# Batches 1 to 3 of a retention kernel: k-v products column-tiled, and the state by one scan per head pair

## The chip, the cores and the metric

One core of a Trainium2 chip runs the kernel. The metric is the device time in microseconds (us), as a median over runs. The profile is one execution of the same program, taken by the hardware profiler; its span goes from the first to the last instruction.

## The reference

Inputs are q, k, v of shape (4 batches, 8 heads, 768 steps, 64), and two weights of 512x2048 and 2048x512. All arithmetic of the reference is in float32.

```python
gamma = 1.0 - 2.0 ** (-5.0 - np.arange(H))
for t in range(S):
    state = gamma[None, :, None, None] * state + np.einsum('bhd,bhe->bhde', k[:, :, t], v[:, :, t])
    y[:, :, t] = scale * np.einsum('bhd,bhde->bhe', q[:, :, t], state)
x = y.transpose(0, 2, 1, 3).reshape(B, S, H * D)
X = np.fft.fft(np.fft.fft(x, axis=1), axis=2)
u = x + np.real(X)
un = (u - u.mean(-1, keepdims=True)) / np.sqrt(u.var(-1, keepdims=True) + 1e-06)
out = u + np.maximum(un @ w_ch1, 0.0) @ w_ch2
```

So there is a decayed linear attention ("retention"), a Fourier mix over steps and channels, a normalisation, and a feed-forward with a ReLU.

## The kernel before

**Tiles.** The 768 steps are cut into NCH = 6 chunks of 128. Two heads form a pair; a batch has four pairs, taken in the order of `PAIR_ORDER`. Within a chunk the attention is computed as a masked product; from chunk to chunk goes a state of 64x64 per head. The kernel works in float16 with float32 sums in PSUM.

**One pair of a later batch (1, 2, 3)** goes through these units, which are Python closures, one after the other over successive steps of `attn_steps`:

- `cast_unit`: GpSimd (in batches 2 and 3 ScalarE for q) casts q, k and v to float16; k is scaled by the decay within its chunk (`kd`).
- `kv_unit`: for chunks 0 to 4, the product of kd and v (128 steps contracted), then the running state `s16`, in which each chunk's product is added to gamma^128 times the state before. TensorE and VectorE (DVE) work here, lines 579 to 597.
- `t_unit`: q and k are transposed, by TensorE in batch 1 and by DMA transposes in batches 2 and 3. qT is zero-padded: for each head, the 64 rows of the other head of the pair are zero.
- `a_unit`: k times q per chunk (line 566), then the mask with its decay on DVE (line 568).
- `y_unit`: per head, q times the state of the chunk before (line 615) and the masked product times v (line 619) add up in one PSUM tile; ScalarE scales it into `x` (line 627).

`kv_unit` is emitted one step after the casts and `y_unit` one step after that. The folds (`fold_s`, `fold_d`), the two stages of the Fourier mix (`s1_unit`, `s2_unit`), the normalisation (`norm_unit`, `unT_unit`) and the feed-forward (`h_unit` line 855 and its ReLUs in lines 859 and 861; `ch_unit` line 892 and its last step in line 896) follow.

**The first batch** has units of its own. There, `kv0_unit` computes the products column-tiled: each head has a half of TensorE's columns, and writes 64 of the 128 PSUM partitions. It puts the chunk index innermost, so that the products of one element over five chunks lie side by side in PSUM. `sc_unit` then makes all five states with one `tensor_tensor_scan`; its factors lie in `gk5`, filled by `gk_unit` for all four pairs, with a zero at chunk 0, at which the scan starts afresh. `yx_unit` (line 492) reads the state with a stride of five, row-tiled: each head uses 64 of the array's rows.

**Order.** While the feed-forward of batch b runs, the attention of batch b + 1 is emitted beside it: `emit` merges streams of units by a position between b and b + 1. The first batch is pinned in its order by `pin`; of the later ones only GpSimd's early instructions are, and the framework's scheduler settles the order of the other engines' instructions from estimated costs. Across the first batch, `filler` (line 139) puts dummy matmuls between the units.

**Buffers.** `ps_g` gives five PSUM buffers of one bank to products, transposes, masked products, y and the Fourier stages. `ps_pm` has three, for the feed-forward. `s16` has two buffers in SBUF, kd three, v16 four.

Of the kernel before, what the change touches and what calls it, by code (L numbers as in the profile page):

```python
# [12 lines left out]
ALU = mybir.AluOpType  # L13
f32 = mybir.dt.float32
f16 = mybir.dt.float16
# [3 lines left out]
P = 128  # L19
B, H, S, D = 4, 8, 768, 64  # L20
DM = 512
DFF = 2048
NCH = S // P
# [6 lines left out]
PAIR_ORDER = [0, 1, 3, 2]  # L30
# [4 lines left out]
def kernel(  # L35
# [9 lines left out]
    nc = tc.nc  # L45
# [3 lines left out]
    def pool(name, bufs, **kw):  # L49
        return ctx.enter_context(tc.tile_pool(name=name, bufs=bufs, **kw))  # L50
# [7 lines left out]
    sp = pool("sp", 2)  # L58
# [8 lines left out]
    ps_g = pool("ps_g", 5, space=PSUM)  # L67
# [3 lines left out]
    ps_pm = None  # L71
# [11 lines left out]
    gkrow = const.tile([P, NHP, NCH - 1], f32, tag="gkrow")  # L83
    gk5 = const.tile([P, NHP, D, NCH - 1], f32, tag="gk5")
# [101 lines left out]
    for h in range(H):  # L186
# [6 lines left out]
                            op0=ALU.mult)  # L193
# [262 lines left out]
    def sc_unit(i):  # L456
        def run():
            st = at[0, i]
            st["s16"] = sp.tile([P, D, NCH - 1], f16, tag="s16", name="s16",
                                padded_shape=[P, P, NCH - 1])  # L460
            nc.vector.tensor_tensor_scan(
                out=st["s16"].rearrange("p e c -> p (e c)"),
                data0=gk5[:, PAIR_ORDER[i]].rearrange("p e c -> p (e c)"),
                data1=st["wkf"], initial=0.0, op0=ALU.mult, op1=ALU.add)
        return run
# [108 lines left out]
    def kv_unit(b, i):  # L574
        def run():
            st = at[b, i]
            hp = PAIR_ORDER[i]
            kd, v16 = kd_of[b, i], v16_of[b, i]
            s16 = sp.tile([P, NCH - 1, P], f16, tag="s16", name="s16")
            st["s16"] = s16  # L580
            for c0, n in ((0, 3), (3, 2)):
                wk = ps_g.tile([P, 3, P], f32, tag="g", name="wkK", padded_shape=[P, 4, P])
                for c in range(c0, c0 + n):
                    nc.tensor.matmul(wk[:, c - c0, :], kd[:, c].rearrange("p a b -> p (a b)"),
                                     v16[:, c].rearrange("p a b -> p (a b)"),
                                     start=True, stop=True)
                for c in range(c0, c0 + n):
                    if c == 0:
                        if b == 0:
                            nc.scalar.copy(s16[:, 0], wk[:, 0])  # L590
                        else:
                            nc.vector.tensor_copy(s16[:, 0], wk[:, 0])
                    else:
                        nc.vector.scalar_tensor_tensor(out=s16[:, c], in0=s16[:, c - 1],  # L594
                                                       scalar=gkrow[:, hp, 1:2],
                                                       in1=wk[:, c - c0],
                                                       op0=ALU.mult, op1=ALU.add)
        return run

    def y_unit(b, i):  # L600
        def run():
            st = at.pop((b, i))
            hp = PAIR_ORDER[i]
            v16, s16, atm, qT = v16_of[b, i], st["s16"], st["atm"], st["qT"]
            ypool, ytag = (ps_pm, "pm") if b == 0 else (ps_g, "g")
            yk = [ypool.tile([P, NCH, D], f32, tag=ytag, name="wkY", padded_shape=[P, 8, D])
                  for _ in range(2)]
            for c in range(1, NCH):
                for h2 in range(2):
                    sl = slice(64 * h2, 64 * h2 + 64)  # L610
                    if b == 0:
                        lhsT, rhs = qT[sl, c, :], s16[sl, c - 1, sl]
                    else:
                        lhsT, rhs = qT[:, h2, c, :], s16[:, c - 1, sl]
                    nc.tensor.matmul(yk[h2][:, c, :], lhsT, rhs,
                                     start=(c == 1), stop=False, skip_group_check=True)
            for h2 in range(2):
                for c in range(NCH):
                    nc.tensor.matmul(yk[h2][:, c, :], atm[:, c, h2, :], v16[:, c, h2, :],  # L619
                                     start=False, stop=(c == NCH - 1), skip_group_check=True)  # L620
                h = 2 * hp + h2
                x = xts[b % 2]
                if h < 4:
                    dst = x[:, :, 0, 64 * h + 1:64 * h + 65]
                else:
                    dst = x[:, :, 1, 513 - 64 * h:449 - 64 * h:-1]
                nc.scalar.activation(dst, yk[h2], AF.Copy, bias=0.0, scale=gq8[:, h:h + 1])  # L627
        return run
# [390 lines left out]
    ps_pm = pool("ps_pm", 3, space=PSUM)  # L1019
    late_consts()  # L1020
    streams = []
    for b in range(B):
# [17 lines left out]
        if b + 1 < B:  # L1040
# [6 lines left out]
            else:  # L1047
                streams.append(([load_unit(b + 1, i) for i in range(4)], b - 0.3, b + 0.15))
                n = [len(u) for u in steps]
# [40 lines left out]
```

## Time and profile before

| | |
|---|---|
| median of 3 runs | 263.74 us (262.87 to 264.59) |
| the profiled execution's own time | 263.17 us |
| its span | 261.5 us |
| granted TensorE clock, mean | 0.997 |
| PE busy | 241.9 us (93%) |
| DVE busy | 182.9 us (70%) |
| ACT busy | 117.5 us (45%) |
| POOL busy | 72.7 us (28%) |

PE is TensorE, DVE is VectorE, ACT is ScalarE, POOL is GpSimd; PEld is the loading of weights into TensorE, beside its matmuls. L594 is line 594 of the kernel. In a group of instructions, the tiles written stand before the arrow and the tiles read after it, then the shape, the count, the busy time in us with the mean duration in ns, and the idle time of the engine just before with what ended it. Matmuls overlap: the duration of one is its time from start to end, while the next may start much earlier, so what a matmul costs TensorE is the distance from its start to the next one's. A row of the timeline merges instructions of one line; its second number reaches from the first start to the last end.

### The profile page before, as it was taken

The numbers are of one execution on the slowest core, as the hardware profiler recorded it, in microseconds if no ns is written. First come the engines' busy times: TensorE is split into PE (matmuls) and PEld (weight loads), VectorE is DVE, ScalarE is ACT, GpSimd is POOL, SyncE is SP. The second block draws the span as 40 slices with busy tenths as digits, with TensorE's granted clock in tenths as the row PEclk, the third lists the DMA queues.
The fourth block names the chain that finished last, engine by engine and source line by source line (L and its number), as shares of the span: only waits on it lengthen the run. The fifth ranks groups of instructions, "written<-read, shape, count | busy, mean of one in ns | idle before, by whom it ended". The sixth has DMA issues, their size and how long they took to land.

```text
span 261.5 us, 5242 instructions
## 1 busy us (share of the span) xinstructions
PE 241.9 (93%) x2024; PEld 146.1 (56%) x2024; DVE 182.9 (70%) x446; ACT 117.5 (45%) x242; POOL 72.7 (28%) x129
## 2 busy tenths in 40 slices
PE   6897899989998989799999999899999999999993
PEld 2454778756766536465566546555556455545541
DVE  7999857878999775898777726897687637523421
ACT  7877677653652346653144406551245305402200
POOL 6658301586100081570001603550002203100000
PEclk9999999999999999999999999999999999999998
DMA  8998999999999109999990294686110431211012
GB/s 177 265 247 136 204 202 213 228 241 260 270 225 216 46 0 236 170 201 188 260 235 2 41 173 122 129 112 131 43 40 0 53 116 35 43 66 55 0 43 80
DMA packets 97432, 35.99 MB, mean 138 GB/s; under 512 B 88192, under 2 KB 94336, under 8 KB 97408
## 3 DMA queue, kind: packets, MB, share of 16 engines
q1 hardware_dynamic: 93184, 31.47, 58.9%
q0 software_dynamic: 4224, 4.19, 9.9%
q8 instruction: 16, 0.26, 0.4%
q14 instruction: 8, 0.07, 0.1%
HBM read 27.26 MB, written 6.29 MB: 128 GB/s over the span
## 4 chain that ended last, share of the span: by engine, by line
PE 48%; DVE 18%; ACT 9%; DMA 9%; POOL 7%; SPq 4%; issue 3%; POOLq 0%; ACTq 0%
PE psc L892 19%; PE psh L855 16%; DMA qTz<-q16z 4%; SPq L153 4%; POOL u L795 3%; ACT x L627 3%; DVE bst L811 3%; DVE atm L568 3%; PE ps L685 2%; DMA unT<-un 2%; DMA k<-in_k_dram 2%; DVE xab L644 2%; PE wkA L566 2%; DVE ht L861 2%; POOL u L793 2%
## 5 line engine op out<-in xcount | busy, mean ns | idle before, releaser
L892 PE MATMUL psc<-w,ht 128*128 128x512 f16 x384 | 89.7, 379 | 0.0
L855 PE MATMUL psh<-unT,w 128*128 128x384 f16 x448 | 82.7, 326 | 2.0 <-ACT ht L859 1.1
L855 PEld LDWEIGHTS <-w 128*128 128x128 f16 x448 | 42.5, 98 | 26.2 <-issue 3.3
L892 PEld LDWEIGHTS <-ht 128*128 128x128 f16 x384 | 36.4, 98 | 36.7
L859 ACT ACTIVATE ht<-psh 128x384 f16<-128x384 f32 x56 | 27.4, 488 | 54.3 <-PE psh L855 54.3
L793 POOL TENSOR_TENSOR u<-u,x 128x256 f32<-128x256 f32 x21 | 13.3, 635 | 126.6 <-DVE u L786 123.0
L861 DVE TENSOR_SCALAR ht<-psh 128x384 f16<-128x384 f32 x56 | 30.8, 550 | 12.1 <-PE psh L855 11.8
L896 DVE SCALAR_TENSOR_TENSOR ob<-psc,stats,u 128x512 f32<-128x512 f32 x24 | 17.9, 746 | 25.9 <-PE psc L892 25.8
L568 DVE TENSOR_TENSOR atm<-wkA,maskp 128x512 f16<-128x512 f32 x36 | 23.6, 680 | 2.0 <-PE wkA L566 2.0
L627 ACT ACTIVATE x<-wkY,gexp 128x384 f16<-128x384 f32 x24 | 12.8, 580 | 22.7 <-PE wkY L619 22.6
L813 ACT ACTIVATE un<-u,stats 128x512 f16<-128x512 f32 x21 | 15.1, 720 | 15.8 <-DVE stats L812 13.0
L811 DVE BATCH_NORM_STATS2 bst<-u 128x6 f32<-128x512 f32 x21 | 14.6, 694 | 9.4 <-POOL u L795 9.3
L594 DVE SCALAR_TENSOR_TENSOR s<-s,gkrow,wkK 128x128 f16<-128x128 f16 x48 | 16.3, 339 | 1.1
L139 PE MATMUL wps<-ht 128*128 128x512 f16 x44 | 14.4, 434 | 2.2 <-POOL ht L184 2.2
L566 PE MATMUL wkA<-qTz,kT 128*128 128x256 f16 x72 | 12.6, 272 | 3.1 <-DMA qTz<-q16z 2.9
L349 POOL TENSOR_SCALAR kd<-k,gexp 128x384 f16<-128x384 f32 x24 | 13.7, 583 | 1.7 <-DMA k<-in_k_dram 1.7
L795 POOL TENSOR_TENSOR u<-u,x 128x256 f32<-128x256 f32 x21 | 13.3, 634 | 2.4 <-DVE u L788 1.3
L786 DVE SCALAR_TENSOR_TENSOR u<-pq,g,qn 128x257 f32<-128x257 f32 x24 | 11.4, 474 | 3.5 <-ACT qn L783 3.5
L872 PE MATMUL psh<-unT,w 128*128 128x128 f16 x192 | 11.4, 219 | 0.4 <-ACT unT L846 0.2
L566 PEld LDWEIGHTS <-kT 128*128 128x128 f16 x72 | 6.8, 97 | 8.6 <-issue 4.6
L783 ACT COPY qn<-pq 128x255 f32<-128x255 f32 x24 | 8.8, 369 | 6.2 <-PE pq L774 5.4
L872 PEld LDWEIGHTS <-w 128*128 128x128 f16 x192 | 11.0, 98 | 0.8 <-issue 0.7
(142 smaller groups left out, 314.5 us busy)
## 6 DMA issues: line engine op xcount, KB each, us to landing
q<-in_q_dram SPq DMA_DIRECT2D x16, 384.0 KB, 6.0
k<-in_k_dram SPq DMA_DIRECT2D x16, 384.0 KB, 5.7
v<-in_v_dram SPq DMA_DIRECT2D x16, 384.0 KB, 6.3
out_dram<-ob SPq DMA_DIRECT2D x24, 256.0 KB, 2.2
w<-in_moe_w_ch_dram POOLq DMA_DIRECT2D x8, 512.0 KB, 11.1
unT<-un SPq DMA_TRANSPOSE x12, 2.5
kT<-kd SPq DMA_TRANSPOSE x8, 3.1
qTz<-q16z SPq DMA_TRANSPOSE x8, 3.8
```

Source lines behind the costliest of these rows:

```text
L566: nc.tensor.matmul(wk[:, c2], st["kT"][:, c, :], st["qT"][:, :, c, :], start=True, stop=True)
L568: nc.vector.tensor_tensor(out=st["atm"][:, 2 * part:2 * part + 2], in0=wk, in1=maskp[:, PAIR_ORDER[i]].unsqueeze(1).to_broadcast([P, 2, 2, ...
L627: nc.scalar.activation(dst, yk[h2], AF.Copy, bias=0.0, scale=gq8[:, h:h + 1])
L793: nc.gpsimd.tensor_tensor(out=u[:, kb, 0:256], in0=u[:, kb, 0:256], in1=x[:, kb, 0, 1:257], op=ALU.add)
L795: nc.gpsimd.tensor_tensor(out=u[:, kb, 256:512], in0=u[:, kb, 256:512], in1=x[:, kb, 1, 257:1:-1], op=ALU.add)
L811: nc.vector.bn_stats(bst, u[:, kb, :])
L855: nc.tensor.matmul(psh, w116[:, cb, fb * P:(fb + 1) * P], unT[:, cb, rt * 384:(rt + 1) * 384], start=(cb == 0), stop=(cb == 3))
L859: nc.scalar.activation(ht16[:, fb, :], psh, AF.Relu, bias=0.0, scale=-1.0)
L861: nc.vector.tensor_scalar(out=ht16[:, fb, :], in0=psh, scalar1=-1.0, scalar2=0.0, op0=ALU.mult, op1=ALU.max)
L872: nc.tensor.matmul(psh[:, f], w116[:, cb, fb * P:(fb + 1) * P], unT[:, cb, kb * P:(kb + 1) * P], start=(cb == 0), stop=(cb == 3))
L892: nc.tensor.matmul(psc, ht16[:, fb, rb3 * P:(rb3 + 1) * P], w216[:, fb, :], start=(fb == 0), stop=(fb == NFB - 1))
L896: nc.vector.scalar_tensor_tensor(out=ob, in0=psc, scalar=lb[b]["st"][:, rb, 3:4], in1=lb[b]["u"][:, rb, :], op0=ALU.mult, op1=ALU.add)
```

## The change

For batches 1 to 3, `kv_unit` now does what `kv0_unit` and `sc_unit` do. Ten matmuls per pair (five chunks, two heads) of 128 rows by 64 columns with 64 moving columns go column-tiled into one PSUM tile of [128, 64, 5]; before, five matmuls of 128x128 with 128 moving columns went into two PSUM tiles, in which only the diagonal blocks were of use. One scan makes the state `s16` as [128, 64, 5]; before, it was a copy and four `scalar_tensor_tensor` steps into [128, 5, 128]. `y_unit` reads `s16[:, :, c - 1]`, 64 columns with a stride of five elements; before, it read 64 contiguous ones, `s16[:, c - 1, sl]`. The stationary side, the zero-padded qT, is as it was. Branches for batch 0, which these units do not serve, are taken out, and so is the padding of `s16` in the first batch.

```diff
@@ sc_unit
             st["s16"] = sp.tile([P, D, NCH - 1], f16, tag="s16", name="s16",
-                                padded_shape=[P, P, NCH - 1])
+)
@@ kv_unit
-            hp = PAIR_ORDER[i]
             kd, v16 = kd_of[b, i], v16_of[b, i]
-            s16 = sp.tile([P, NCH - 1, P], f16, tag="s16", name="s16")
-            st["s16"] = s16
-            for c0, n in ((0, 3), (3, 2)):
-                wk = ps_g.tile([P, 3, P], f32, tag="g", name="wkK", padded_shape=[P, 4, P])
-                for c in range(c0, c0 + n):
-                    nc.tensor.matmul(wk[:, c - c0, :], kd[:, c].rearrange("p a b -> p (a b)"),
-                                     v16[:, c].rearrange("p a b -> p (a b)"),
-                                     start=True, stop=True)
-                for c in range(c0, c0 + n):
-                    if c == 0:
-                        if b == 0:
-                            nc.scalar.copy(s16[:, 0], wk[:, 0])
-                        else:
-                            nc.vector.tensor_copy(s16[:, 0], wk[:, 0])
-                    else:
-                        nc.vector.scalar_tensor_tensor(out=s16[:, c], in0=s16[:, c - 1],
-                                                       scalar=gkrow[:, hp, 1:2],
-                                                       in1=wk[:, c - c0],
-                                                       op0=ALU.mult, op1=ALU.add)
+            wkf = ps_g.tile([P, D * (NCH - 1)], f32, tag="g", name="wkK", padded_shape=[P, DM])
+            wk = wkf.rearrange("p (e c) -> p e c", c=NCH - 1)
+            for c in range(NCH - 1):
+                for h2 in range(2):
+                    nc.tensor.matmul(wk[D * h2:D * h2 + D, :, c], kd[:, c, h2, :],
+                                     v16[:, c, h2, :], start=True, stop=True)
+            st["s16"] = sp.tile([P, D, NCH - 1], f16, tag="s16", name="s16")
+            nc.vector.tensor_tensor_scan(
+                out=st["s16"].rearrange("p e c -> p (e c)"),
+                data0=gk5[:, PAIR_ORDER[i]].rearrange("p e c -> p (e c)"),
+                data1=wkf, initial=0.0, op0=ALU.mult, op1=ALU.add)
@@ y_unit
-            ypool, ytag = (ps_pm, "pm") if b == 0 else (ps_g, "g")
-            yk = [ypool.tile([P, NCH, D], f32, tag=ytag, name="wkY", padded_shape=[P, 8, D])
+            yk = [ps_g.tile([P, NCH, D], f32, tag="g", name="wkY", padded_shape=[P, 8, D])
                   for _ in range(2)]
             for c in range(1, NCH):
                 for h2 in range(2):
-                    sl = slice(64 * h2, 64 * h2 + 64)
-                    if b == 0:
-                        lhsT, rhs = qT[sl, c, :], s16[sl, c - 1, sl]
-                    else:
-                        lhsT, rhs = qT[:, h2, c, :], s16[:, c - 1, sl]
-                    nc.tensor.matmul(yk[h2][:, c, :], lhsT, rhs,
+                    nc.tensor.matmul(yk[h2][:, c, :], qT[:, h2, c, :], s16[:, :, c - 1],
                                      start=(c == 1), stop=False, skip_group_check=True)
```

## The prediction

> **What bounds the kernel now.** I read the page first, then the busy time by stage, then the waits of TensorE, then the groups of instructions, and last the timeline of TensorE around single units.
>
> ```profile
> PE 241.9 (93%) x2024; PEld 146.1 (56%) x2024; DVE 182.9 (70%) x446; ACT 117.5 (45%) x242; POOL 72.7 (28%) x129
> ```
>
> TensorE is busy for 93% of the span. An average says little about the stages that the edit touches, so I cut out the three in which attention of batches 1, 2 and 3 runs beside the feed-forward of the batch before (columns: stretch, its length, busy us and instructions of PE, PEld, DVE, ACT, POOL).
>
> ```profile
> 60.00:100.00 40.00, 37.83 (x340) 23.47 (x338) 33.55 (x79) 16.84 (x32) 9.46 (x15) 1.00 0.81 164
> 100.00:140.00 40.00, 37.77 (x335) 23.89 (x333) 31.88 (x79) 18.66 (x39) 9.41 (x15) 1.00 1.08 206
> 158.00:198.00 40.00, 37.66 (x325) 23.27 (x323) 31.94 (x78) 17.46 (x38) 9.42 (x15) 1.00 0.46 91
> ```
>
> In each, PE idles only 2.2 to 2.3 us of 40, some 6.7 us in all, while DVE has 6 to 8 us to spare. Whatever lightens DVE can be paid out only from PE's idle time. Who causes that idle time (PE's waits over the whole span: us, times, longest)?
>
> ```profile
> PE wkA L566 <- DMA qTz<-q16z: 2.9, 3, 1.5
> ...
> PE ps L685 <- DVE eo L654: 1.0, 4, 0.5
> ...
> PE psh L855 <- DVE ht L861: 0.5, 3, 0.2
> ...
> PE wkY L615 <- DVE g L692: 0.2, 1, 0.2
> ```
>
> The largest wait of these stages is for the DMA transposes of q, which the edit doesn't touch. Waits for DVE add up to 1.7 us, part of it in the first batch. The chain that ended last gives 18% to DVE, but much of this lies beside a busy PE, so I do not read it as 18% to be won.
>
> **What the Trainium skill says.** "TensorEngine Tiling (Array Packing)", Key Properties: changing the tiling mode drains TensorE. "Advanced Engine Details and Errata", Memory Cachelines: SBUF is read in 16-byte lines, and an access to another line each time is penalised; for PSUM, a non-contiguous pattern slows matmuls. "TensorE: Matmul & The Clock Gate", Back-to-back issue gap: up to 64 columns the gap is at a floor of about 25 ns. The trace agrees with all three where the first batch does what the later ones now are to do: a drain on both sides of the column-tiled unit, 70 ns between strided pairs, and 30 ns for contiguous 64-column matmuls.
>
> **The change on DVE.** The groups (busy us, mean ns of one):
>
> ```profile
> L594 DVE SCALAR_TENSOR_TENSOR s<-s,gkrow,wkK 128x128 f16<-128x128 f16 x48 | 16.3, 339 | 1.1
> L592 DVE CAST s<-wkK 128x128 f16<-128x128 f32 x12 | 3.4, 283 | 1.2 <-PE wkK L584 1.0
> L461 DVE TENSOR_TENSOR_SCAN s<-gk,wkK 128x320 f16<-128x320 f32 x4 | 3.2, 808 | 0.0
> ```
>
> Removed per head pair: one cast of 283 ns and four steps of 339 ns, 1.64 us. Added: one scan of 808 ns, the same shape as line 461. That is 0.83 us less for each of 12 pairs, 10.0 us of DVE. Its worth is what PE waits for DVE. Of the 1.7 us above, with what comes through ACT from DVE's statistics and through PSUM buffers, between 0 and about 3 us could go; I take 1.5. Other edits with one answer: the padding of s16 is gone (SBUF only, nothing); one PSUM buffer per pair instead of two (in the 1.5); gk5 is there for all pairs since the first batch (nothing). No DMA is added or moved. The only new wait is that the scan needs all ten products instead of the first three; its reader is y_unit, one step later, so this is covered by the work of a whole step. A scan holds DVE for 0.8 us at a stretch, so a ReLU behind it is at most 0.5 us later than behind one 339 ns step; psh has three buffers as cover, and I cost it at nothing.
>
> **The change on PE: the products.** The timeline of PE (start, us, line, count) around a unit of the first batch and one of a later batch:
>
> ```profile
> 13.81 0.33 PE L430 MATMUL wkA<-qTz,kT 64*128 64x128 f16 x6
> 14.07 0.39 PE L139 MATMUL wps<-ht 128*128 128x512 f16 x1
> 14.39 0.47 PE L452 MATMUL wkK<-v,kd 128*64 128x64 f16 x10
> 14.79 0.51 PE L405 MATMUL tq<-ident,q16z 128*128 128x128 f16 x6
> ```
>
> ```profile
> 63.57 0.38 PE L892 MATMUL psc<-w,ht 128*128 128x512 f16 x1
> 63.78 0.44 PE L584 MATMUL wkK<-v,kd 128*128 128x128 f16 x5
> 64.06 0.45 PE L615 MATMUL wkY<-s,qTz 128*128 128x64 f16 x10
> 64.36 0.51 PE L619 MATMUL wkY<-v,atm 128*128 128x64 f16 x12
> ```
>
> Durations overlap, so I price by starts. The untiled unit takes 63.78 to 64.06, 0.28 us for five matmuls. The tiled one takes 14.39 to 14.79, 0.40 us for ten: five pairs side by side, then a pause before the full array is used again. A 512-column matmul holds PE for 0.21 us (63.57 to 63.78), but the one ahead of the tiled unit holds it for 0.32 us (14.07 to 14.39), so 0.10 us more goes on entry. Together 0.50 against 0.28, +0.22 us, x12 = +2.6 us. In the first batch such pauses lie among filler matmuls (line 139); in the later batches they lie between feed-forward matmuls that are all on the path. Below: at least the +0.12 us per pair without the entry (+1.4 us); above: +5.2 us if the order puts other work into the middle of each unit and drains twice.
>
> **The change on PE: reading the state.** y_unit keeps ten full-array matmuls of 64 columns per pair, but the moving operand becomes s16[:, :, c-1], one f16 in every five (10 bytes). Before, these cost 64.06 to 64.36, 0.30 us for ten, 30 ns each. No full-array strided row exists in the trace. The nearest is line 492, the same read, but row-tiled in pairs:
>
> ```profile
> 12.64 0.53 PE L492 MATMUL wkY<-s,qTz 64*128 64x64 f16 x10
> 13.09 0.61 PE L139 MATMUL wps<-ht 128*128 128x512 f16 x2
> ```
>
> 0.53 us less one latency of about 0.25 leaves 0.28 us for four steps from pair to pair: 70 ns. Row tiling is not what makes it slow: the contiguous row-tiled pairs of line 430 with twice the columns step in (0.33 - 0.22) / 2 = 56 ns. A pair runs at once on different partitions, so 70 ns is what 64 strided columns take. In the later batches the two heads of a pair use the whole array one after the other, so each of the ten pays it alone. Bounds: 30 ns (stride harmless, +0), 35 ns (the pair shared one read, +0.6 us), 70 ns (+40 ns x 120 = +4.8 us). I take 70, as the contiguous pair leaves little else to explain it. Less than nothing is excluded, since the matmuls stay as many and as long.
>
> **Sum.** +2.6 + 4.8 - 1.5 = +5.9 us. The profiled execution took 263.17 us (span 261.5 and 1.7 around it), so 269.1 us on its scale; it lies 0.57 us below the median 263.74, so 269.6 us as a median. Nearly all of the +7.4 us counts, as PE has 6% idle there and its longest waits are for transposes issued behind its own progress.
>
> **The rivals.**
>
> A, the forecast: both prices on PE, 269.6 us (own range 267.8 to 271.5).
>
> B, the stride is harmless on the full array: 263.74 + 2.6 + 0.6 - 1.5 = 265.4 us. For it: the 70 ns are seen only in row-tiled pairs. Against: line 430.
>
> C, faster: DVE is the hidden limit. ReLU outputs, masks and PSUM buffers come free sooner, all through the attention stages, and of the 7.8 us that PE idles between 52 and 198 us (6.7 as above and 1.1 before 60) 5.5 go. With harmless strides, 263.74 + 2.6 - 5.5 = 260.8 us. It decides only if the stride is free and more than 2.6 us of idle time hangs on DVE. For it: DVE's 33.55 of 40 us and its share of the chain. Against: the waits name a DMA first, and DVE for 1.7 us.
>
> D, the new lengths change the order: the instructions of the later batches are not pinned, and order follows estimated costs. Tiled units split by other matmuls drain again, +2.6 us, or a transpose falls later by about 1 us: 269.6 + 2.6 + 1 = 273.2 us. For it: y units are already split in the trace (line 615 in fives). Against: the five products of a pair stay together, and they are now in one PSUM buffer. That the change doesn't do what it says at all I leave out: the scan and the tiled form run in this trace already.
>
> **How the numbers follow.** A 0.68, B 0.17, C 0.05, D 0.10. About 1% can be told from no change here, that is 261.1 to 266.4 us. B lies mostly within: same 0.11, and its upper part goes to slower; slower 0.84, faster 0.05. The range 265.2 to 272.8 leaves out C, the lower half of B and most of D.
>
> **What would show it.** Right: DVE busy near 173 us with 12 more scans of about 0.8 us; the group of y's state matmuls stepping by 70 ns (0.65 to 0.75 us for ten); 0.10 us more on the matmul ahead of each product unit and 0.40 us from it to the next; PE busy a higher share of a longer span. Wrong: steps of 30 ns in y (then B), PE idle in the three stages falling by over 4 us (C), product units in pieces or longer waits for qTz (D).

## The result: slower by 1.4%, in direction and mechanism as forecast, with less of the cost arriving than the sum said

The changed kernel took 267.02 us (266.78 to 267.74, 4 runs), the kernel before 263.33 us in the same comparison: a ratio of 1.0137, 95% interval 1.0094 to 1.0180. The forecast was +5.9 us; it is +3.7. The profiled execution took 267.74 us, its span is 266.0 us; it is the slowest of the four.

The page of the changed kernel, busy time of each engine:

```profile
PE 247.8 (93%) x2084; PEld 150.9 (57%) x2084; DVE 176.5 (66%) x398; ACT 117.5 (44%) x242; POOL 72.8 (27%) x129
```

TensorE has 5.9 us more, DVE 6.4 us less. The same three stages of 40 us (length, then busy us and instructions of PE, PEld, DVE, ACT, POOL):

```profile
60.00:100.00 40.00, 38.59 (x350) 24.32 (x347) 31.05 (x63) 16.96 (x31) 9.27 (x14) 1.00 0.74 156
100.00:140.00 40.00, 37.62 (x337) 24.08 (x338) 27.29 (x57) 16.85 (x38) 9.45 (x15) 1.00 1.13 210
158.00:198.00 40.00, 38.72 (x330) 23.83 (x329) 26.39 (x54) 15.86 (x34) 9.43 (x15) 1.00 0.48 108
```

DVE now has 9 to 14 us of 40 to spare, where it had 6 to 8. TensorE is as full as before: a little fuller in two of the three stages. The groups of the new instructions:

```profile
L585 DVE TENSOR_TENSOR_SCAN s<-gk,wkK 128x320 f16<-128x320 f32 x12 | 9.8, 814 | 2.3 <-PE wkK L582 2.1
L582 PE MATMUL wkK<-v,kd 128*64 128x64 f16 x120 | 5.6, 246 | 0.0
L600 PE MATMUL wkY<-s,qTz 128*128 128x64 f16 x120 | 10.9, 250 | 0.1
```

And the timeline of TensorE around one pair, to be read by starts:

```profile
62.59 1.89 PE L877 MATMUL psc<-w,ht 128*128 128x512 f16 x8
64.41 0.47 PE L582 MATMUL wkK<-v,kd 128*64 128x64 f16 x10
64.81 0.89 PE L600 MATMUL wkY<-s,qTz 128*128 128x64 f16 x10
65.52 0.53 PE L604 MATMUL wkY<-v,atm 128*128 128x64 f16 x12
```

Eight matmuls of 512 columns take 62.59 to 64.41, 1.82 us, where eight steps of 0.216 would be 1.73: 0.09 us to enter the tiled mode. The products take 64.41 to 64.81, 0.40 us. The reads of the state take 64.81 to 65.52, 0.71 us, where they took 0.30. All three are the numbers of the forecast.

What did not follow it is the waiting. I took, from the traces, the distance from each matmul's start to the next one's, from 44 us into the span on, and subtracted the usual step (the median) of that kind of matmul and the pauses around the tiled units; what is left is waiting. It is 14.3 us before and 10.7 us after. TensorE's own work grew by 7.9 us (3.0 for entering and leaving the tiled mode, -0.3 for the products themselves, +5.3 for the strided reads; 7.4 was forecast), and 3.6 us of waiting went, where 1.5 was forecast. So the question for the experiments is: what bought those 3.6 us?

Each waiting is that of one execution, and a kernel's profiled execution lies up to 1.0 us off its median (0.7 above it for the changed kernel). By the medians, 7.9 - 3.7 = 4.2 us went, with an interval of about 1.1 us to either side. Differences of this waiting below 1 us decide little by themselves.

### The profile page after: what moved, and what is told of

Its sections match the earlier page's. It is cut to its first block, busy times and chain, and to the rows that moved or that the text cites. A ratio compares the mean times of both kernels' runs of the same rounds, so it can differ in the third digit from the quotient of the medians.

```text
span 266.0 us, 5319 instructions
## 1 busy us (share of the span) xinstructions
PE 247.8 (93%) x2084; PEld 150.9 (57%) x2084; DVE 176.5 (66%) x398; ACT 117.5 (44%) x242; POOL 72.8 (27%) x129
## 4 chain that ended last, share of the span: by engine, by line
PE 59%; DVE 14%; ACT 7%; POOL 6%; DMA 5%; SPq 4%; issue 3%; POOLq 0%; ACTq 0%
PE psc L877 24%; PE psh L840 18%; SPq L153 4%; PE wkY L600 3%; DMA q<-in_q_dram 3%; PE ps L670 3%; POOL u L780 3%; ACT x L612 2%; PE wkA L566 2%; DVE bst L796 2%; DVE xab L629 2%; DMA qTz<-q16z 2%; DVE eo L639 2%; POOL u L778 2%; PE wkK L582 2%
## 5 line engine op out<-in xcount | busy, mean ns | idle before, releaser
L846 DVE TENSOR_SCALAR ht<-psh 128x384 f16<-128x384 f32 x56 | 30.7, 549 | 12.5 <-PE psh L840 12.1
L612 ACT ACTIVATE x<-wkY,gexp 128x384 f16<-128x384 f32 x24 | 12.7, 581 | 26.1 <-PE wkY L604 26.1
L566 PE MATMUL wkA<-qTz,kT 128*128 128x256 f16 x72 | 12.7, 272 | 2.8 <-DMA qTz<-q16z 2.8
L629 DVE TENSOR_TENSOR xab<-x 128x780 f16<-128x780 f16 (+4 forms) x18 | 8.8, 522 | 6.7 <-ACT x L612 5.5
```

What stands on the lines that cost most here:

```text
L566: nc.tensor.matmul(wk[:, c2], st["kT"][:, c, :], st["qT"][:, :, c, :], start=True, stop=True)
L846: nc.vector.tensor_scalar(out=ht16[:, fb, :], in0=psh, scalar1=-1.0, scalar2=0.0, op0=ALU.mult, op1=ALU.max)
```

## The experiments

Waiting is worked out as above; own work is TensorE's, against the kernel before; DVE is the busy time of the page. Every ratio is to the kernel before, run on the same chip.

| kernel | own work, us | DVE, us | waiting, us | median, us | ratio (95%) |
|---|---|---|---|---|---|
| before | 0 | 182.9 | 14.3 | 263.33 | 1 |
| changed | +7.9 | 176.5 | 10.7 | 267.02 | 1.0137 (1.0094 to 1.0180) |
| contiguous read | +2.7 | 175.9 | 11.8 | 263.31 | 1.0000 (0.9985 to 1.0016) |
| scan twice | +7.9 | 184.4 | 10.4 | 267.57 | 1.0188 (1.0158 to 1.0218) |
| stride, slowed steps | +5.3 | 192.8 | 14.5 | 268.22 | 1.0195 (1.0176 to 1.0215) |
| PSUM contiguous | +6.5 | 175.5 | 10.6 | 266.25 | 1.0136 (1.0106 to 1.0166) |
| before in new order | 0 | 185.6 | 15.9 | 264.86 | 1.0062 (1.0043 to 1.0081) |
| changed in old order | +7.9 | 176.8 | 11.2 | 267.02 | 1.0126 (1.0079 to 1.0173) |
| two buffers | +8 | 176.6 | 9.9 | 266.86 | 1.0138 (1.0091 to 1.0185) |
| tiled with steps | +1.5 | 180.4 | 12.7 | 262.60 | 0.9982 (0.9964 to 1.0000) |
| stride, DVE untouched | +5.3 | 183.0 | 12.1 | 266.21 | 1.0127 (1.0107 to 1.0147) |
| light DVE | 0 | 176.6 | 13.2 | 262.37 | 0.9966 (0.9951 to 0.9982) |
| two pairs together | 0 | 178.6 | 22.1 | 270.52 | 1.0276 (1.0247 to 1.0305) |
| cast on ScalarE | +1.5 | 177.9 | 11.9 | 262.34 | 0.9954 (0.9937 to 0.9971) |

### The strided read taken out

```diff
-nc.tensor.matmul(yk[h2][:, c, :], qT[:, h2, c, :], s16[:, :, c - 1],
+s16 = st["s16"].rearrange("p e c -> p (e c)").rearrange("p (c e) -> p c e", c=NCH - 1)
+nc.tensor.matmul(yk[h2][:, c, :], qT[:, h2, c, :], s16[:, c - 1, :],
```

> The changed kernel, but y_unit reads the scan's output as [5, 64] with 64 contiguous elements per chunk; the scan still writes [64, 5], so the states that y reads are mixed up, with the work otherwise the same. Steps between y's state matmuls should fall from 73 to 29 ns, 120 x 44 ns = 5.3 us less on TensorE. Theory relief (the 3.6 us of waiting that TensorE lost in the changed kernel were bought by DVE's 10 us): the waits stay as small, 267.0 - 5.3 = 261.7 us. Theory cover (those waits shrank because TensorE, with 7.5 us more of its own work, came to them later): with 2.6 us of added work left, about a third of the 3.6 us stays away, 263.3 + 2.6 - 1.3 = 264.6 us. If the stride were harmless on the full array: 267.0 us.

Measured: 263.31 us, level with the kernel before. Its timeline, for the same stretch of a pair:

```profile
64.18 0.47 PE L582 MATMUL wkK<-v,kd 128*64 128x64 f16 x10
64.58 0.47 PE L601 MATMUL wkY<-s,qTz 128*128 128x64 f16 x10
64.88 0.51 PE L605 MATMUL wkY<-v,atm 128*128 128x64 f16 x12
```

The reads are back at 0.30 us for ten (64.58 to 64.88), with TensorE, DVE and ScalarE in the order of the changed kernel: the stride alone makes the difference, on the full array too, and rival B falls. The time lies between the two theories, 1.6 above relief and 1.3 below cover. The column tiling (+2.7 of own work) is paid by 2.5 us less of waiting.

### DVE's load put back

```diff
+for _ in range(2):
     nc.vector.tensor_tensor_scan(out=st["s16"]..., data1=wkf, ...)
```

> The changed kernel with every scan of batches 1 to 3 done twice into the same tile: 12 x 0.81 = 9.7 us more on DVE, so that its load is again that of the kernel before, with TensorE's work as in the changed kernel. Theory relief: TensorE's waits come back, 267.0 + 3.6 = 270.6 us, at least 269. Theory cover: DVE has the room, 266.5 to 267.5 us.

Measured: 267.57 us. DVE is busy for 184.4 us, as in the kernel before, and TensorE's waiting did not come back (10.4 us). The theory that DVE's lightness bought all of it (at least 269 us) is refuted. That it bought a part is not: the ratio is higher than that of the changed kernel by half a per cent, 1.3 us, with intervals that overlap. Nor is DVE's load the only difference: the scheduler put 13 of TensorE's 1924 matmuls other than k-v products at another place than in the changed kernel.

### The stride alone, in the kernel before

```diff
-s16 = sp.tile([P, NCH - 1, P], f16, tag="s16", name="s16")
+s16 = sp.tile([P, P, NCH - 1], f16, tag="s16", name="s16")
-nc.vector.tensor_copy(s16[:, 0], wk[:, 0])
+nc.vector.tensor_copy(s16[:, :, 0], wk[:, 0])
-nc.vector.scalar_tensor_tensor(out=s16[:, c], in0=s16[:, c - 1], ...
+nc.vector.scalar_tensor_tensor(out=s16[:, :, c], in0=s16[:, :, c - 1], ...
-lhsT, rhs = qT[:, h2, c, :], s16[:, c - 1, sl]
+lhsT, rhs = qT[:, h2, c, :], s16[:, sl, c - 1]
```

> The kernel before (untiled products, copy and four steps on DVE), with s16 laid out as [128, 5], so that y_unit reads it with the stride of the changed kernel. TensorE +5.3 us (120 x 44 ns), DVE's steps the same in number and size; their own strided writes are expected to cost under 0.05 us each. Theory relief: nothing is taken off DVE, so the waits stay, 263.3 + 5.3 = 268.6 us. Theory cover: two thirds of the added work, so some 2.4 us of the waits are covered, 266.2 us.

Measured: 268.22 us, +5.1, as if nothing were covered. But the run was not what I meant it to be: the steps on DVE slowed down with their strided operands, from 339 to 566 ns, and the cast from 283 to 509.

```profile
L594 DVE SCALAR_TENSOR_TENSOR s<-s,gkrow,wkK 128x128 f16<-128x128 f16 x48 | 27.2, 566 | 1.1
```

Ten us more on DVE and 5.3 us more on TensorE were changed together, so this run alone decides nothing; the run with DVE untouched, below, is its clean form. The order on TensorE, DVE and ScalarE is that of the kernel before in both.

### The PSUM layout

```diff
-wk = wkf.rearrange("p (e c) -> p e c", c=NCH - 1)
+wk = wkf.rearrange("p (c e) -> p c e", c=NCH - 1)
-nc.tensor.matmul(wk[D * h2:D * h2 + D, :, c], ...
+nc.tensor.matmul(wk[D * h2:D * h2 + D, c, :], ...
```

> The changed kernel with the tiled products written to PSUM as [5, 64], contiguous per chunk, and not with a stride of 20 bytes; the scan reads the same bytes in the same flat order, so the states are mixed up, with the work otherwise the same. If the steps of 56 ns from pair to pair come from loading weights: same steps, 267.0 us under either theory. If the strided PSUM write sets them: down to about 30 ns, 48 x 26 ns = 1.2 us less, 265.8 us.

The timeline around one unit:

```profile
57.95 0.35 PE L582 MATMUL wkK<-v,kd 128*64 128x64 f16 x10
58.23 1.04 PE L877 MATMUL psc<-w,ht 128*128 128x512 f16 x4
```

Ten products take 0.28 us and not 0.40, with 32 ns from pair to pair and not 56. So the strided write to PSUM set the step, not the loading of weights, and it cost 0.12 us per pair, 1.4 us in all. The median is 0.8 us below that of the changed kernel, but the ratio to the kernel before is the same (1.0136 and 1.0137): the gain is shown in the trace, not in the time.

### The order of the instructions

The scheduler gave the changed kernel another order: of TensorE's 1924 matmuls other than k-v products, 41 stand elsewhere in the traces when they are told apart by their tiles. Each kernel was held to the order of the other:

```diff
 emit(streams)
+for eng, order in ORDER.items():
+    seq = [x for x in tc.nc.cur_bb.bb.instructions if str(x.engine).split(".")[-1] == eng]
+    for m, n in zip(order, order[1:]):
+        tc.add_manual_dep(seq[n], seq[m].name, ...)
```

> The kernel before, with all its work, buffers and DVE steps, but TensorE, DVE and ScalarE held to the order that the scheduler gave to the changed kernel (each instruction behind the one ahead of it in that order; a pair's five products where the ten stood, its cast and four steps where the scan stood). Theory order (the 3.5 us of waiting went because the scheduler, with other lengths, put other instructions first): 263.2 - 3.5 = 259.7 us. Theory buffers (one PSUM buffer per pair instead of two) and theory chain (one DVE instruction instead of five): the waits stay, 263.2 us, within 0.7.

> The changed kernel held to the order of the kernel before on TensorE, DVE and ScalarE (a pair's ten products where the five stood, its scan where the cast stood). Theory order: the waits come back, 266.8 + 3.5 = 270.3 us. Theories buffers and chain: 266.8 us, within 0.7.

The kernel before in the new order took 264.86 us, with more waiting (15.9 us) and not less; the changed kernel in the old order took 267.02 us, with 11.2 us. So the new order is not what took the waiting away. It is not without effect: in it, the kernel before is slower by 0.6%, 1.6 us. (A pair's steps on DVE are held together there, which may be a part of it.) Rival D is refuted for this change: the changed kernel takes as long in the old order, and in its own order all 12 product units stay whole.

### The PSUM buffers

```diff
+wkd = ps_g.tile([P, DM], f32, tag="g", name="wkD")
+nc.tensor.matmul(wkd[0:D, 0:1], kd[:, 4, 0, :], v16[:, 4, 0, 0:1], start=True, stop=True)
 nc.vector.tensor_tensor_scan(...)
+nc.vector.tensor_copy(junk[0:D], wkd[0:D, 0:1])
```

> The changed kernel with a second PSUM buffer of ps_g taken by each pair: one tiled matmul of one column writes it, and a DVE copy of one column after the scan lets go of it (12 x some 0.05 us on TensorE and 0.06 us on DVE). Theory buffers: the waits come back, 270 us. Theories order and chain: 267.3 us; the scheduler's order is nearly that of the changed kernel.

Measured: 266.86 us. Its ratio is that of the changed kernel (1.0138 and 1.0137). A second buffer per pair changes nothing that can be told; the theory of the buffers is refuted.

### Tiled products with the old steps

```diff
-wk = wkf.rearrange("p (e c) -> p e c", c=NCH - 1)
+wk = ps_g.tile([P, NCH - 1, D], f32, tag="g", name="wkK", padded_shape=[P, 8, D])
...
-nc.vector.tensor_tensor_scan(...)
+nc.vector.tensor_copy(s16[:, 0], wk[:, 0])
+for c in range(1, NCH - 1):
+    nc.vector.scalar_tensor_tensor(out=s16[:, c], in0=s16[:, c - 1],
+                                   scalar=gkrow[:, hp, 1:2], in1=wk[:, c],
+                                   op0=ALU.mult, op1=ALU.add)
```

> The changed kernel with the products still column-tiled in one PSUM buffer, but laid out as [5, 64], and the state made by a copy and four steps of 64 columns instead of the scan, into [5, 64], so that y_unit reads contiguously. TensorE's work against the kernel before: +2.7 for the tiling, -1.4 for the contiguous PSUM writes, 0 for the reads. Theory chain: the waits of the kernel before, 263.2 + 1.3 = 264.5 us. Theory buffers: 3.5 us less of them, 261.0 us. Theory order: the scheduler gives a third order here, so anything between.

Measured: 262.60 us, between the theories of chain and buffers, and 12.7 us of waiting. The steps on the half-width tile are shorter than those of the kernel before (275 against 339 ns):

```profile
L587 DVE SCALAR_TENSOR_TENSOR s<-s,gkrow,wkK 128x64 f16<-128x64 f16 x48 | 13.2, 275 | 1.0
```

TensorE does 1.5 us more than before and the kernel is not slower: with reads and writes contiguous, 1.6 us less of waiting pays for the tiled mode. How much of that is lighter steps, cover or the third order, this run does not tell.

### Cover alone, and a lighter DVE

Here the two causes are tried one by one. First the stride in the kernel before, with DVE's steps and the order of all engines untouched:

```diff
+s16 = s16.rearrange("p c e -> p (c e)").rearrange("p (e c) -> p e c", c=NCH - 1)
-lhsT, rhs = qT[:, h2, c, :], s16[:, c - 1, sl]
+lhsT, rhs = qT[:, h2, c, :], s16[:, sl, c - 1]
```

> The kernel before, with s16 still written contiguously by the same cast and steps, but read by y_unit as if it were [128, 5], with a stride of five; the states are mixed up, the work on DVE is that of the kernel before, TensorE has 5.3 us more, and the order of all engines is that of the kernel before. Theory cover (with more work of its own, TensorE comes later to what it waits for): some 1.5 us of waiting go, 263.0 + 3.8 = 266.8 us, as against the stride with slowed steps, which gave +5.1. Theory lighter DVE (only less work on DVE shortens the waits): 263.0 + 5.3 = 268.3 us.

Measured: 266.21 us, +3.1 against its before of 263.14. Own work +5.3, waiting -2.2, in the same order on TensorE, DVE and ScalarE: cover is shown. It can be seen in single waits. In the kernel before:

```profile
175.19 0.46 PE L615 MATMUL wkY<-s,qTz 128*128 128x64 f16 x10
175.48 0.40 PE L619 MATMUL wkY<-v,atm 128*128 128x64 f16 x8
...
176.05 1.03 PE L892 MATMUL psc<-w,ht 128*128 128x512 f16 x4
177.55 0.38 PE L566 MATMUL wkA<-qTz,kT 128*128 128x256 f16 x2 [0.47 <-DMA qTz<-q16z]
```

With the strided read, in the same order:

```profile
177.60 0.90 PE L616 MATMUL wkY<-s,qTz 128*128 128x64 f16 x10
178.32 0.42 PE L620 MATMUL wkY<-v,atm 128*128 128x64 f16 x8
...
178.90 1.03 PE L893 MATMUL psc<-w,ht 128*128 128x512 f16 x4
179.97 0.38 PE L566 MATMUL wkA<-qTz,kT 128*128 128x256 f16 x2
```

Four matmuls of 512 columns need 0.86 us. Before, the next matmul starts 1.50 us after they began: 0.64 us of waiting for a DMA transpose. With the strided read it is 1.07 us: 0.21 us of waiting. The reads of the state ahead of them grew by 0.43 us (0.29 to 0.72), and the wait shrank by as much. This y unit's extra time cost nothing at all, since the transpose was already under way: it was issued at 172.02 us before and at 174.43 us here, ahead of the y unit in both.

Then a lighter DVE, with TensorE's work untouched:

```diff
-for c in range(c0, c0 + n):
-    ... cast for c == 0, scalar_tensor_tensor for the others
+nc.vector.tensor_copy(s16[:, c0:c0 + n], wk[:, 0:n])
```

> The kernel before, with two casts in place of a cast and four steps: each PSUM tile of products is copied to s16 whole, and the decayed sum over chunks is left out. Some 0.7 to 0.9 us less on DVE per pair, 8 to 11 us in all, with TensorE's work unchanged. Theory lighter DVE: 2 to 3.5 us of TensorE's waits go, 259.5 to 261 us. Theory cover: 263.0 us, within 0.5.

Measured: 262.37 us, ratio 0.9966 (0.9951 to 0.9982): 0.9 us less for 6.3 us less on DVE, and 1.1 us less of waiting. That is less than either number that I had given it. But DVE is not all that changed here. The scheduler gave this run an order of its own: 36 of TensorE's 1924 matmuls other than k-v products stand elsewhere than before, and only 9 elsewhere than in the changed kernel. The kernel before, held to the changed kernel's order, had a ratio of 1.0062; against that, the light DVE gains 1.0%, some 2.5 us, though there a pair's steps on DVE are also held together. So relief is real, and worth between 0.9 and 2.5 us by these runs.

The feed-forward's matmuls show where a lighter DVE helps. The idle time ahead of them (last column) before, with the stride alone, with the light DVE and in the changed kernel:

```profile
L855 PE MATMUL psh<-unT,w 128*128 128x384 f16 x448 | 82.7, 326 | 2.0 <-ACT ht L859 1.1
L856 PE MATMUL psh<-unT,w 128*128 128x384 f16 x448 | 82.6, 326 | 1.7 <-ACT ht L860 0.6
L845 PE MATMUL psh<-unT,w 128*128 128x384 f16 x448 | 82.1, 326 | 1.1 <-DMA unT<-un 0.6
L840 PE MATMUL psh<-unT,w 128*128 128x384 f16 x448 | 82.4, 326 | 0.6 <-DVE ht L846 0.4
```

These waits went mostly where DVE was lighter, and hardly with more work on TensorE alone. (In the changed kernel in the old order they are 1.3 us, so the order has a share in them.) With the light DVE, the waits ahead of y's matmuls grew from 0.5 to 1.8 us at the same time. They are 2.6 us in the kernel before in the new order, 1.4 us in the changed kernel with the contiguous read, and 0.4 us in the changed kernel: there the strided reads cover them.

Cover and relief, 2.2 + 1.1 = 3.3 us, come near the 3.6 in question, but that does not show the split. The changed kernel has 7.9 us of added work to cover with, not 5.3, and the light DVE has another order. The run with slowed steps gives relief a weight of its own: against the run with DVE untouched, in the same order, 9.8 us more on DVE brought 2.4 us of waiting back. The run with the scan done twice does not fit: it put 7.9 us on DVE and brought none back in its profile. There the load comes as one longer stretch behind the products, and not as steps between other work; that this is the reason was not tried. So both causes are shown, and how they share the 3.6 us of the changed kernel stays open.

### Two versions that might beat both

Products of two pairs back to back, so that the mode changes six times and not twelve:

```diff
-if 0 <= i < 4:
-    un.append(kv_unit(b, i))
+if step in (2, 4):
+    un += [kv_unit(b, step - 2), kv_unit(b, step - 1)]
-sp = pool("sp", 2)
+sp = pool("sp", 3)
...
```

in the version with tiled products and steps, and TensorE's order given, with the first pair's products moved directly ahead of the second's.

> The tiled products with a cast and four steps of 64 columns, and contiguous reads and writes (262.6 us), with the products of two pairs back to back on TensorE: pairs 0 and 1, and 2 and 3, one step later for the even ones; s16 has three buffers. Six changes of the tiling mode and back instead of twelve, each 0.09 + 0.15 us: 1.5 us less, 261.1 us. If the later products delay y, or two chains behind one another on DVE do: 262.6 us or more.

Measured: 270.52 us. TensorE's own work fell as planned, and its waiting rose to 22.1 us. (A small part of both can be the clock: its granted mean was 0.990 in the profiled execution; the one execution at 0.999 took 268.75 us.) The waits of the kernel, of two engines:

```profile
PE wkA L566 <- DMA qTz<-q16z: 4.9, 3, 2.3
PE pst L828 <- ACT un L799: 2.4, 2, 1.7
...
ACT x L613 <- PE wkY L605: 24.6, 9, 10.4
```

y comes later: the longest wait of ScalarE for it went from 5.4 us in the kernel before to 10.4 us. TensorE waits for the transposes into qTz for 4.9 us where it was 2.9. That these are late because y lets go of their buffer late is likely, but the profile does not name it. TensorE's own work was not dearer; the place of the work was worth more than its drains.

The other moves the cast of chunk 0 from DVE to ScalarE, in the version with tiled products and steps:

```diff
-nc.vector.tensor_copy(s16[:, 0], wk[:, 0])
+nc.scalar.copy(s16[:, 0], wk[:, 0])
```

> The tiled products with contiguous reads and writes and four steps of 64 columns, with the cast of chunk 0 on ScalarE instead of DVE: DVE 12 x 0.22 = 2.6 us less, TensorE's work the same. By the light-DVE run (6.3 us less on DVE gave 0.9 us), 0.4 us less than the 262.6 us with the cast on DVE: 262.2 us, or 0.9965 of the kernel before. If ScalarE gets to the cast late, the steps on DVE queue behind it and wait: 262.6 us or more.

```profile
L585 ACT CAST s<-wkK 128x64 f16<-128x64 f32 x12 | 2.5, 212 | 13.0 <-issue 8.5 <-PE wkK L583 3.8 <-ACT ht L845 0.7
L587 DVE SCALAR_TENSOR_TENSOR s<-s,gkrow,wkK 128x64 f16<-128x64 f16 x48 | 13.2, 275 | 3.4 <-ACT s L585 2.7
```

Measured: 262.34 us against 263.34, ratio 0.9954 (0.9937 to 0.9971). DVE now waits 2.7 us for ScalarE's cast (second row, last column). This version is faster than both kernels. That moving the cast pays by itself is not shown: the interval overlaps that of the version with the cast on DVE (0.9964 to 1.0000).

## Why the prediction was right, and where its sum was off

- **What bounds the kernel.** Right. TensorE's starts and steps explain the added work. But the 6.7 us of idle time, as the pool from which refunds come, were read from busy time, in which a matmul of 512 columns counts with its 379 ns and not with its step of 216 ns, so that short waits vanish. By starts, TensorE waits for some 11 us in those three stages.
- **The products, +2.6 us.** Right, in the trace: 3.0 us for entering and leaving less 0.3 us. The cause inside the unit was more than the mode: the step of 56 ns between pairs is the strided PSUM write, as the run with the contiguous layout shows.
- **The strided read, +4.8 us.** Right: 73 ns a step, 0.71 us for ten, +5.3 us. The reading from the row-tiled line 492 carried over to the full array, and rival B, that it would not, is refuted by the contiguous read (263.31 us).
- **"Nearly all of the +7.4 us counts."** This is the step that failed. I argued that the longest waits are for transposes issued behind TensorE's own progress. The wait shown above isn't moved as a whole: the transpose is under way, and what TensorE does more in the meantime is taken from the wait. The stride with DVE untouched shows 2.2 us so covered of 5.3 us. The term was set at about zero.
- **The worth of DVE's relief, 1.5 us.** Right in kind, and not contradicted in size: the light DVE shows 0.9 us for nearly the same relief, and up to 2.5 us at nearly the same order. The whole refund was 3.6 us and not 1.5, because cover comes on top. The forecast of +5.9 us stayed near enough because the refund is small beside the two prices on TensorE, which were right.
- **DVE's saving, 10.0 us.** The durations of the state's instructions did fall by 9.9 us (19.7 to 9.8), but the busy time by only 6.4, and I had forecast 173 us where it is 176.5. Neighbouring instructions can overlap: three masks of 680 ns take 1.88 us in the trace of before. Over all of DVE, the sum of durations is 22.6 us above the busy time before and 19.6 us above it after, so 3.0 us of what was taken out had run beside other instructions; the durations of the others grew by 0.5 us. The steps on the state do not overlap one another, only their neighbours.
- **Rivals.** C, that DVE is the hidden limit, is refuted by the light DVE: 0.3%, or 1.0% at nearly the same order, not the 2.1% or more that would have been needed. D, the order, is refuted by both exchanges of it.

## What to carry to other kernels

A form of a computation taken over from a place where an engine has filler around it must be priced anew where that engine is the bound: price each of its parts (mode changes, strided reads, strided writes) by the distance between starts at the place where it already runs. Then ask for each wait of the bound engine whether its releaser is already under way: if it is, added work ahead of it is free up to the length of the wait. Work taken away there can come back as waiting: taking out the strided read (5.2 us of own work) brought 1.1 us of it. Where an engine's instructions overlap, price what is taken out by the busy time that goes, not by the sum of durations. And look at the order that the scheduler gave before calling a run a change of one thing.

## What the runs showed of the hardware that I had not expected

- A column-tiled pair of 64-column matmuls steps in 56 ns when PSUM is written with a stride of 20 bytes, in 32 ns when it is written contiguously.
- 64 moving columns of float16 with a stride of 10 bytes step in 73 ns on the full array, against 29 ns contiguous; row-tiled pairs with the same stride step in 70 ns.
- A `scalar_tensor_tensor` of 128x128 with a float16 operand and a float16 output at a stride of 10 bytes takes 566 ns and not 339, a cast of the same size 509 and not 283. The scan of 320 elements takes 814 ns; it reads and writes contiguously.
